# Sliding-window attention and a gated FFN: split float32r scores from unit 16 on, raw weights in buffers of their own

## The chip, the cores and the metric

The kernel runs on one core of a Trainium2 chip. The metric is device time in microseconds of one launch, median of three runs. TensorE is called PE in the profile (PEld is its weight load), VectorE DVE, ScalarE ACT, GpSimd POOL, SyncE SP. Each engine runs its own list of instructions in order; SP issues most of the DMA transfers and holds up those behind one that waits.

## The reference

Attention over four batches of 8 heads, 768 positions and 64 dimensions, with 8 global keys and a window of 96, then one FFN on its output with a rational activation. The weights come as float64.

```python
scores = scale * np.matmul(q, k.transpose(0, 1, 3, 2))
...
bias = -slopes[:, None, None] * dist[None, :, :]
scores = np.where(keep, scores + bias, -1e9)          # keep: global or in the window
a = softmax(scores)
x = np.matmul(a, v)                                   # (3072 tokens, 512)
...
h = x @ w_in                                          # (512, 2048)
g = (a0 + a1*h + a2*h**2 + a3*h**3) / (1 + |b0|*|h| + |b1|*h**2 + 1e-6)
return g @ w_out                                      # (2048, 512)
```

## The kernel before

**Units.** The work of attention is cut into 96 units: 128 queries of two heads. Unit u belongs to chunk `c = u // 8` of 256 tokens; eight units, two rows of 128 queries (t = 0, 1) by four head pairs (p = 0 to 3), make a chunk. A row's keys are its own 128 and the 128 before, with the global keys copied into the first 8 columns of the older block. Row i is 0 to 5 in a batch, so units 0 to 23 are the first batch, and units 16 to 23 are its rows 4 and 5.

**Two forms of scores.** Units below `PLAIN` (24) compute in float32: two transposes on PE (`tk`, q and k of a head pair, L389), ACT copies them to `qz` and `kF` (L402, L404), two float32 matmuls give the scores (`s`, L433). From unit 24 on every operand is split into two float32r parts. `st_move` (L147) sends the loaded q and k of two units through a DMA into a float32r tile `mv`; PE transposes it (L383); ACT writes the rounded half of each head into `kq` (L415) and DVE the remainder (L416) into the other half of the partitions; two DMAs turn the halves of q around (`qT`, L420 and L421); then four float32r matmuls give the scores (L438). The keys of the row before are kept in `kF` or in `kq`, the global keys in `kGF` or `kG`.

**After the scores.** DVE takes masked scores with their maximum (`pr`, L452), ACT the exponential, DVE the sums (L467, L469), POOL multiplies by the reciprocal (L478); PE transposes the probabilities (`tp`, L494), ACT or DVE copies them to `pT`; PE multiplies by v (`o`, L520), and ACT and DVE write the result into `xh` and `xl`. For units from 24 on, the probabilities pass through one more DMA (`pm`) and are transposed in float32r.

**FFN.** It is cut into 96 tiles f of 256 of the 2048 columns by 256 tokens, eight to a chunk. Tiles 0 to 7 (chunk 0) use float32 matmuls (`h` at L263, `acc` at L342), the others three float32r matmuls for each product (L271, L347), with weights split into a high part (`hi`, ACT or DVE) and a low part (`win_l`, `wout_l`, mostly POOL, L223). The activation of a tile is `st_ew1` to `st_ew4`: ACT's `fu`, `fa`, `fs`, DVE's polynomial (L302, L303), POOL's sum (L304), ACT's logarithm and exponential (L311, L312), and DVE's last three steps L316, L317, L318, after which PE may accumulate it.

**Weights.** A piece of 128 rows by 512 weights arrives as float64 (512 KB, `fetch`, L183) in a buffer r, and `decode` makes float32 of it in four steps: ACT (L202), POOL (L206), DVE twice (L207, L209). There are 32 pieces, in the order of the table `WSCHED`. Six raw buffers: three in the pool `early`, three that belong to tag g, which the FFN uses later.

**Order.** The loop over steps t writes each stage with a priority out of the tables `PRI` and `PRI_A`, and a scheduler orders each engine's list by these priorities and its own estimates. FFN tile f stands at step `turn(f)`: f + 10 up to f = 16, then slowly up to f + 13. At t = `PLAIN` the pool `early` is closed and the pool of the split form opened in its place.

Of the kernel before, what the change touches and what calls it, by code (L numbers as in the profile page):

```python
# [18 lines left out]
P = 128  # L19
G = 8  # L20
# [6 lines left out]
EARLY_LAG = 10  # L27
F2 = 2
# [6 lines left out]
PLAIN = 24  # L35
# [71 lines left out]
def tile_kernel(ctx: ExitStack, tc: tile.TileContext, q, k, v, n_global, n_local,  # L107
# [49 lines left out]
    wout_l = const.tile([P, NFT, DM], FR, name="wout_l")  # L157
# [8 lines left out]
    def w_lo(key):  # L166
        if key[0]:
            return win_l[:, key[1], key[2] * 2 * TOK:(key[2] + 1) * 2 * TOK]
        return wout_l[:, key[1], :]
# [225 lines left out]
    def st_qkE(u):  # L395
# [14 lines left out]
        raw = tk.bitcast(F32)  # L410
        half = float(2.0 ** (p - 1))
        for x in range(2):
            own, other = slice(x * D, (x + 1) * D), slice((1 - x) * D, (2 - x) * D)
            at = kq[:, 2 * p + x, i % 2:3:2 - i % 2, :]
            nc.scalar.activation(out=at[own], in_=raw[own], func=AF.Copy, scale=half)  # L415
            nc.vector.scalar_tensor_tensor(out=at[other], in0=raw[own], scalar=half, in1=at[own], op0=ALU.mult,  # L416
                                           op1=ALU.subtract)
        hs = slice(2 * p, 2 * p + 2)
        qT = pl.late.tile([P, 2, P], FR, tag="qT", name=f"qT{u}", bufs=4)
# [51 lines left out]
    def st_norm(u):  # L471
        if u < DIVIDED:
            return
        i = unit(u)[4]
        pr, st = prob[u]
        for x in range(2):
            d = blocks_of(pr[:, x], i)
            nc.gpsimd.tensor_scalar(  # L478
                out=d, in0=d, scalar1=st[:, 6 + x:7 + x], scalar2=None, op0=ALU.mult)
        if u >= PLAIN:  # L480
            own = (lambda y: y) if i else (lambda y: y[:, :, 0, :])
            moved = pl.late.tile([P, 2, 2, P], FR, tag="pm", name=f"pm{u}", bufs=2)
            nc.sync.dma_start(out=own(moved).bitcast(F32), in_=own(pr))
            prob[u] = (moved, st)

    def st_pT(u):
# [3 lines left out]
        kind, unit_r = (FR, ident_r) if u >= PLAIN else (F32, ident)  # L490
# [9 lines left out]
    def run_of(u):  # L500
        return 4 if u >= PLAIN else 2
# [26 lines left out]
    def st_x(u0):  # L528
# [16 lines left out]
        if u0 < DIVIDED:  # L545
            rs = pl.early.tile([P, 2, P], F32, tag="rs", name=f"rs{u0}", bufs=1)
            nc.scalar.copy(out=rs, in_=r)
            nc.vector.tensor_tensor(out=o, in0=o, in1=rs, op=ALU.mult)
# [7 lines left out]
    def windowed(lates):  # L556
# [3 lines left out]
        pl.kF = pl.early.tile([P, NPAIR, 2, P], F32, name="kF")  # L560
# [278 lines left out]
```

## Time and profile before

| | |
|---|---|
| runs | 749.71, 750.93, 751.01 us; median 750.93 |
| profiled execution | 749.57 us, of it span 747.8 us |
| mean granted PE clock | 0.996 |
| busy share of the span | PE 97%, PEld 84%, DVE 80%, ACT 77%, POOL 61% |
| DMA | 79.49 MB, 0.9 or more busy in the first 40 us, 0.3 to 0.5 from 160 to 660 us |

Busy shares are means over stages that differ: up to some 90 us weights are fetched and decoded, while attention of the first two chunks and the float32 tiles of the FFN run; weights are split up to some 180 us; then all chunks look alike up to 660 us, and the rest is FFN alone. A row of the chain is a start, a length, the engine, the tile and the line. A timeline row has in brackets how long the engine idled before it, and what ended that.

### The profile page before, as it was taken

To read this page: it belongs to the slowest core of one execution; us is meant where nothing else is said; L and a number is where in the kernel's file an instruction comes from. 1 tells how busy PE (TensorE), PEld (TensorE's weight loads), DVE (VectorE), ACT (ScalarE), POOL (GpSimd) and SP (SyncE) were. 2 spreads that over 40 slices of the span, in tenths; PEclk is the share of its full clock that TensorE was granted. 3 is DMA by queue.
4 is the path that set the end of the run, shared out by engine and by line. 5 is a ranking of instruction groups with operands and counts; after the bars stand their busy time and mean duration, and the time that the engine had idled before them with its cause. 6 is when DMAs were issued, how large, how long until landed. Compare 5 with 4: busy or idle time off the path is not lost.

```text
span 747.8 us, 15330 instructions
## 1 busy us (share of the span) xinstructions
PE 724.8 (97%) x5026; PEld 629.7 (84%) x5026; DVE 601.3 (80%) x1437; ACT 577.1 (77%) x1303; POOL 457.3 (61%) x504
## 2 busy tenths in 40 slices
PE   6798999999999999999999999999999999999996
PEld 4575667888988989998999999998998989998994
DVE  6889975888889897888888888887888888875664
ACT  6898576877977886877887878877877878866764
POOL 3385996776576675655665657656666566664441
PEclk9999999999999999999999999999999999999999
DMA  9986101123534443334334334334434333210000
GB/s 264 299 285 224 43 22 23 50 58 100 142 106 132 146 117 90 114 107 109 111 100 114 114 103 124 116 101 100 123 91 123 117 91 102 77 48 1 29 1 33
DMA packets 123581, 79.49 MB, mean 106 GB/s; under 512 B 82532, under 2 KB 104036, under 8 KB 123492
## 3 DMA queue, kind: packets, MB, share of 16 engines
q1 hardware_dynamic: 122432, 78.15, 36.4%
q8 instruction: 42, 0.69, 0.4%
q10 hardware_dynamic: 1060, 0.26, 0.2%
q14 instruction: 47, 0.39, 0.2%
HBM read 35.92 MB, written 6.29 MB: 56 GB/s over the span
## 4 chain that ended last, share of the span: by engine, by line
PE 87%; DVE 4%; ACT 4%; DMA 2%; issue 1%; POOL 0%; SPq 0%; DVEq 0%; ACTq 0%; POOLq 0%
PE h L271 34%; PE acc L347 32%; PE o L520 5%; PE s L438 5%; PE tp L494 3%; PE acc L342 2%; DMA r<-in_moe_w_in_dram 2%; PE s L433 2%; PE h L263 2%; PE tk L383 1%; ACT pr L462 1%; ACT m L202 1%; DVE pr L452 1%; PE tk L389 0%; ACT fa L296 0%
## 5 line engine op out<-in xcount | busy, mean ns | idle before, releaser
L478 POOL TENSOR_SCALAR pr<-pr,stats 128x256 f32<-128x256 f32 (+1 forms) x176 | 157.0, 903 | 74.0 <-DVE stats L469 47.2
L271 PE MATMUL h<-xh,win_l 128*128 128x256 f32 x704 | 198.2, 282 | 0.0
L304 POOL TENSOR_TENSOR fa<-fa,fs 128x512 f32<-128x512 f32 x95 | 123.8, 1303 | 98.4 <-ACT fs L297 88.0
L347 PE MATMUL acc<-wout_l,g 128*128 128x512 f32 x352 | 139.3, 396 | 0.0
L327 POOL TENSOR_TENSOR g<-fu,g 128x512 fp32r<-128x512 f32 x87 | 114.0, 1311 | 34.3 <-ACT g L326 22.9
L271 PEld LDWEIGHTS h<-xh,win_l 128*128 128x128 f32 x704 | 133.1, 189 | 2.1 <-issue 1.2
L295 ACT ACTIVATE fu<-h,coef 128x512 f32<-128x512 f32 (+1 forms) x97 | 75.1, 774 | 46.4 <-PE h L271 40.9
L462 ACT ACTIVATE pr<-pr,stats 128x256 f32<-128x256 f32 (+1 forms) x192 | 92.9, 487 | 16.8 <-DVE stats L452 16.0
L311 ACT ACTIVATE fs<-fa,coef 128x512 f32<-128x512 f32 (+1 forms) x97 | 69.6, 718 | 30.2 <-POOL fa L304 28.7
L316 DVE SCALAR_TENSOR_TENSOR fu<-fu,coef,q 128x512 f32<-128x512 f32 (+1 forms) x97 | 71.6, 738 | 25.0 <-ACT q L312 23.5
L302 DVE TENSOR_TENSOR fu<-fu,h 128x512 f32<-128x512 f32 (+1 forms) x97 | 65.7, 678 | 30.9 <-ACT fs L297 28.2
L347 PEld LDWEIGHTS acc<-wout_l,g 128*128 128x128 f32 x352 | 66.2, 188 | 11.9
L415 ACT ACTIVATE kq<-tk 64x256 fp32r<-64x256 f32 x144 | 54.3, 377 | 26.5 <-DVE kq L416 15.4
L303 DVE SCALAR_TENSOR_TENSOR fu<-fu,coef,h 128x512 f32<-128x512 f32 (+1 forms) x97 | 71.7, 739 | 1.9
L317 DVE SCALAR_TENSOR_TENSOR q<-fa,coef,q 128x512 f32<-128x512 f32 (+1 forms) x97 | 72.1, 744 | 0.0
L497 DVE COPY pT<-tp 128x512 f32<-128x512 f32 (+1 forms) x75 | 48.4, 645 | 24.9 <-PE tp L494 24.1
L416 DVE SCALAR_TENSOR_TENSOR kq<-tk,kq 64x256 fp32r<-64x256 f32 x144 | 60.9, 423 | 8.7 <-ACT kq L415 4.4
L318 DVE SCALAR_TENSOR_TENSOR fu<-q,fu 128x512 f32<-128x512 f32 (+1 forms) x97 | 66.1, 682 | 1.6
L297 ACT ACTIVATE fs<-h,coef 128x512 f32<-128x512 f32 (+1 forms) x97 | 66.3, 683 | 1.4 <-DVE fu L318 1.1
L296 ACT ACTIVATE fa<-h,coef 128x512 f32<-128x512 f32 (+1 forms) x97 | 65.6, 676 | 0.5 <-DMA out_dram<-o 0.5
L326 ACT CAST g<-fu 128x512 fp32r<-128x512 f32 (+1 forms) x89 | 54.9, 617 | 8.3 <-DVE fu L318 7.6
L312 ACT ACTIVATE q<-fs 128x512 f32<-128x512 f32 (+1 forms) x97 | 57.3, 591 | 1.7 <-DVE fu L318 0.7
(258 smaller groups left out, 2005.6 us busy)
## 6 DMA issues: line engine op xcount, KB each, us to landing
pm<-pr SPq DMA_DIRECT2D x60, 256.0 KB
mv<-nat SPq DMA_DIRECT2D x36, 256.0 KB
qT<-kq SPq DMA_DIRECT2D x144, 64.0 KB
r<-in_moe_w_in_dram SPq DMA_DIRECT2D x16, 512.0 KB
r<-in_moe_w_out_dram SPq DMA_DIRECT2D x16, 512.0 KB
nat<-in_q_dram SPq DMA_DIRECT2D x48, 128.0 KB
vt<-in_v_dram SPq DMA_DIRECT2D x48, 128.0 KB
out_dram<-o SPq DMA_DIRECT2D x24, 256.0 KB
```

The source lines that it names most:

```text
L271: nc.tensor.matmul(out=hps[f][:, y, :], lhsT=w[:, fs], rhs=x[:, ct, :], start=(n == 0), stop=(n == 3 * NCT - 1))
L295: nc.scalar.activation(out=u, in_=h, func=AF.Identity, scale=a3, bias=a2)
L297: nc.scalar.activation(out=s, in_=h, func=AF.Square, scale=b1)
L303: nc.vector.scalar_tensor_tensor(out=u, in0=u, scalar=a1, in1=h, op0=ALU.add, op1=ALU.mult)
L304: side(f).tensor_tensor(out=a, in0=a, in1=s, op=ALU.add)
L311: nc.scalar.activation(out=s, in_=a, func=AF.Ln, bias=q1)
L316: nc.vector.scalar_tensor_tensor(out=u, in0=u, scalar=a0, in1=r, op0=ALU.add, op1=ALU.mult)
L317: nc.vector.scalar_tensor_tensor(out=r, in0=a, scalar=q1, in1=r, op0=ALU.add, op1=ALU.mult)
L327: side(f).tensor_tensor(out=g[:, 1, ys], in0=u, in1=g[:, 0, ys], op=ALU.subtract)
L347: nc.tensor.matmul(out=acc, lhsT=gs[f][:, z, y, ts], rhs=w, start=(ft == 0 and n == 0), stop=(ft == NFT - 1 and n == 2))
L462: nc.scalar.activation(out=d, in_=d, func=AF.Exp, scale=-1.0, bias=st[:, x:x + 1], accum_out=st[:, 2 + 2 * x:3 + 2 * x])
L478: nc.gpsimd.tensor_scalar(out=d, in0=d, scalar1=st[:, 6 + x:7 + x], scalar2=None, op0=ALU.mult)
```

## The change

`PLAIN` is now 16: scores in float32 end after the second row pair of the first batch, and units 16 to 23 use the split form. `MOVED` (24) keeps their probabilities in float32, with their transposes at t - 3 and PV at t - 4. Units 16 to 19 find the keys of the row before in `kF` and split these too (`apart` on `kF`, and a copy of the global keys to `kG`). `turn` spreads its three extra steps as one over tiles 8 to 16 and two over tiles 16 to 24. The pool `share` holds seven buffers of 4 KB a partition for raw weights, which later hold the low parts of w_out, two 128-row blocks each; the eighth pair lies where `kF` was. Raw weights no longer use the g buffers. `MOVED` takes the place of `PLAIN` in the same way in `st_norm` (shown), `st_pT` and `run_of`. A branch that no unit took (in `st_x`) is gone.

```diff
+LATER = ((1, 1), (2, 2))
-PLAIN = 24
+PLAIN = 16
+MOVED = 24
...
-    wout_l = const.tile([P, NFT, DM], FR, name="wout_l")
+    share = ctx.enter_context(tc.tile_pool(name="share", bufs=1))
+    wout_l = {}
...
     def w_lo(key):
-        return wout_l[:, key[1], :]
+        n, m = divmod(key[1], 2)
+        if n not in wout_l:
+            wout_l[n] = shared("k" if n == NFT // 2 - 1 else "s", [P, 2, DM], FR, f"wout_l{n}")
+        return wout_l[n][:, m, :]
+
+    def shared(tag, shape, dt, name):
+        return share.tile(shape, dt, tag=tag, name=name, bufs=1 if tag == "k" else NFT // 2 - 1)
...
-        home = (pl.early, "raw", 3) if (len(full) + len(fetched)) % 6 in (1, 3, 5) else (pl.ffn, "g", pl.gbufs)
-        raw = home[0].tile([P, 2, 2, TOK], F32, tag=home[1], name="r" + "_".join(map(str, key)), bufs=home[2])
+        raw = fetched[key] = shared("s", [P, 2 * TOK, 2], F32, "r" + "_".join(map(str, key)))
...
+        def apart(raw, at):
+            half = float(2.0 ** (p - 1))
+            for x in range(2):
+                own, other = slice(x * D, (x + 1) * D), slice((1 - x) * D, (2 - x) * D)
+                y = at(2 * p + x)
+                nc.scalar.activation(out=y[own], in_=raw[own], func=AF.Copy, scale=half)
+                nc.vector.scalar_tensor_tensor(out=y[other], in0=raw[own], scalar=half, in1=y[own], op0=ALU.mult,
+                                               op1=ALU.subtract)
+        if u < PLAIN + NPAIR:
+            apart(pl.kF[:, p, 1 - i % 2, :], lambda h: kq[:, h, 1 - i % 2, :])
+            nc.gpsimd.tensor_copy(out=pl.kG[:, hs, :], in_=kq[:, hs, 1 - i % 2, 0:G])
+        apart(tk.bitcast(F32), lambda h: kq[:, h, i % 2:3:2 - i % 2, :])
...
-        if u >= PLAIN:
+        if u >= MOVED:
...
-        pl.kF = pl.early.tile([P, NPAIR, 2, P], F32, name="kF")
+        pl.kF = shared("k", [P, NPAIR, 2, P], F32, "kF")
...
-            return f + EARLY_LAG + (LAG - EARLY_LAG) * min(max(f - 2 * FPC, 0), FPC) / FPC
+            return f + EARLY_LAG + sum(n * min(max(f - c * FPC, 0), FPC) / FPC for c, n in LATER)
...
             if t - 2 < PLAIN:
                 on("pT", st_pT, t - 2)
+            elif PLAIN <= t - 3 < MOVED:
+                on("pT", st_pT, t - 3)
...
+            elif t % 2 == 0 and PLAIN <= t - 4 < MOVED:
+                pv(t - 4, 700)
```

Three places in the engines' lists. First DVE while weights are decoded, around the end of FFN tile 1 (names: w1_2_3f is a piece of w_in, w0_10f one of w_out, r its raw form, fu1 and q1 tile 1). Before:

```order
L207 SCALAR_TENSOR_TENSOR w1_2_3f_875<-w1_2_3f_875,r1_2_3_876 128x512
L316 SCALAR_TENSOR_TENSOR fu1_671<-fu1_671,coef_63,q1_747 128x512
L317 SCALAR_TENSOR_TENSOR q1_747<-fa1_672,coef_63,q1_747 128x512
L209 SCALAR_TENSOR_TENSOR w1_0_3f_795<-r1_0_3_796,w1_0_3f_795 128x512
L302 TENSOR_TENSOR fu2_756<-fu2_756,h2_736 128x512
L209 SCALAR_TENSOR_TENSOR w1_1_3f_802<-r1_1_3_803,w1_1_3f_802 128x512
L467 TENSOR_REDUCE stats_64<-stats_64 128x2
L209 SCALAR_TENSOR_TENSOR w1_2_3f_875<-r1_2_3_876,w1_2_3f_875 128x512
L207 SCALAR_TENSOR_TENSOR w1_3_3f_882<-w1_3_3f_882,r1_3_3_883 128x512
L318 SCALAR_TENSOR_TENSOR fu1_671<-q1_747,fu1_671 128x512
```

And now, on the same engine:

```order
L214 SCALAR_TENSOR_TENSOR w1_3_3f_882<-w1_3_3f_882,r1_3_3_883 128x512
L323 SCALAR_TENSOR_TENSOR fu1_673<-fu1_673,coef_65,q1_747 128x512
L324 SCALAR_TENSOR_TENSOR q1_747<-fa1_674,coef_65,q1_747 128x512
L216 SCALAR_TENSOR_TENSOR w1_0_3f_795<-r1_0_3_796,w1_0_3f_795 128x512
L479 TENSOR_REDUCE stats_66<-stats_66 128x2
L216 SCALAR_TENSOR_TENSOR w1_1_3f_802<-r1_1_3_803,w1_1_3f_802 128x512
L214 SCALAR_TENSOR_TENSOR w0_10f_946<-w0_10f_946,r0_10_947 128x512
L216 SCALAR_TENSOR_TENSOR w1_2_3f_875<-r1_2_3_876,w1_2_3f_875 128x512
L216 SCALAR_TENSOR_TENSOR w1_3_3f_882<-r1_3_3_883,w1_3_3f_882 128x512
L309 TENSOR_TENSOR fu2_756<-fu2_756,h2_736 128x512
```

Piece 3_3 moved ahead of tile 1's last three steps, and its second half, the first half of w0_10, the two masked maxima of unit 13 and the first half of w0_11 now stand between L324 and tile 1's last step (L325), which follows these.

Second, PE at the accumulation of FFN tile 5 (`acc0` with `fu5`). Before:

```order
L263 MATMUL h6_1064<-x0_281,w1_2_3f_875 128x256
L263 MATMUL h6_1064<-x0_281,w1_3_3f_882 128x256
L263 MATMUL h7_1138<-x0_281,w1_0_3f_795 128x256
L263 MATMUL h7_1138<-x0_281,w1_1_3f_802 128x256
L263 MATMUL h7_1138<-x0_281,w1_2_3f_875 128x256
L263 MATMUL h7_1138<-x0_281,w1_3_3f_882 128x256
L433 MATMUL s16_1127<-kF_95,qz_97 128x256 x2
L389 MATMUL tk17_1143<-ident_65,nat16_720 128x128 x2
```

Two rows further on stands the accumulation. Now:

```order
L390 MATMUL tk16_1079<-ident_r_68,mv16_1072 128x128 x4
L506 MATMUL tp14_1133<-ident_67,pr14_964 128x128 x4
L349 MATMUL acc0_1_778<-w0_6f_706,fu3_840 128x512
L349 MATMUL acc0_1_778<-w0_7f_714,fu3_840 128x512
L270 MATMUL h7_1162<-x0_283,w1_0_3f_795 128x256
L270 MATMUL h7_1162<-x0_283,w1_1_3f_802 128x256
L270 MATMUL h7_1162<-x0_283,w1_2_3f_875 128x256
L349 MATMUL acc0_0_768<-w0_10f_946,fu5_991 128x512
```

The score block of unit 16 and the second transposes of the pair are gone from here, and the accumulation of tile 5 stands two h matmuls sooner.

Third, DVE ahead of that tile's last steps. Before:

```order
L302 TENSOR_TENSOR fu5_993<-fu5_993,h5_973 128x512
L467 TENSOR_REDUCE stats_64<-stats_64 128x2
L318 SCALAR_TENSOR_TENSOR fu4_925<-q4_984,fu4_925 128x512
L303 SCALAR_TENSOR_TENSOR fu5_993<-fu5_993,coef_63,h5_973 128x512
L469 RECIPROCAL stats_64<-stats_64 128x2
L222 CAST w1_0_1h_1199<-w1_0_1f_322 128x512
L316 SCALAR_TENSOR_TENSOR fu5_993<-fu5_993,coef_63,q5_1075 128x512
```

And now:

```order
L309 TENSOR_TENSOR fu5_991<-fu5_991,h5_971 128x512
L644 TENSOR_SCALAR halves_1068<-masks_70 128x384
L644 TENSOR_SCALAR half0_1069<-mask0_69 128x128
L425 SCALAR_TENSOR_TENSOR kq_1066<-kF_97,kq_1066 64x128 x3
L310 SCALAR_TENSOR_TENSOR fu5_991<-fu5_991,coef_65,h5_971 128x512
L425 SCALAR_TENSOR_TENSOR kq_1066<-kF_97,kq_1066 64x128 x4
L229 CAST w1_0_1h_1215<-w1_0_1f_324 128x512
L425 SCALAR_TENSOR_TENSOR kq_1066<-kF_97,kq_1066 64x128
```

The eight subtractions that split the keys of the row before, and the halving of the masks, came in ahead of tile 5's last three steps.

More of the change, by code (lines that the diff above doesn't have):

```diff
@@ L179, in fetch @@
         src = w_in_i[r, 4 * j * TOK:4 * (j + 1) * TOK] if z else w_out_i[r, :]
-        home = (pl.early, "raw", 3) if (len(full) + len(fetched)) % 6 in (1, 3, 5) else (pl.ffn, "g", pl.gbufs)
-        raw = home[0].tile([P, 2, 2, TOK], F32, tag=home[1], name="r" + "_".join(map(str, key)), bufs=home[2])
-        raw = fetched[key] = raw.rearrange("p z a b -> p (z a b)").rearrange("p (f w) -> p f w", w=2)
+        raw = fetched[key] = shared("s", [P, 2 * TOK, 2], F32, "r" + "_".join(map(str, key)))
         eng.dma_start(out=raw.bitcast(I32), in_=src.rearrange("p (f w) -> p f w", w=2))
@@ L409, in st_qkE @@
         kq = pl.kq
[L410 to L417, printed above, removed]
-        hs = slice(2 * p, 2 * p + 2)
+        hs = slice(2 * p, 2 * p + 2)
+        def apart(raw, at):
[10 more added lines that the diff above has]
+        apart(tk.bitcast(F32), lambda h: kq[:, h, i % 2:3:2 - i % 2, :])
         qT = pl.late.tile([P, 2, P], FR, tag="qT", name=f"qT{u}", bufs=4)
@@ L489, in st_pT @@
         W = 2 if i else 1
-        kind, unit_r = (FR, ident_r) if u >= PLAIN else (F32, ident)
+        kind, unit_r = (FR, ident_r) if u >= MOVED else (F32, ident)
         t_ps = pl.ps_t.tile([P, 2, 2, P], kind, tag="t", name=f"tp{u}")
@@ L500, in run_of @@
     def run_of(u):
-        return 4 if u >= PLAIN else 2
+        return 4 if u >= MOVED else 2
     def st_pv(u0):
@@ L544, in st_x @@
         xh, xl = xT[c]
[L545 to L548, printed above, removed]
         nc.scalar.copy(out=xh[:, ps, cs], in_=o)
@@ L642, in windowed @@
                 on("split", st_move, t + 2)
-            if t - 4 >= PLAIN:
+            if t - 4 >= MOVED:
                 on("qkT", st_pT, t - 4, more=-5)
-            if t % 4 == 0 and t - 8 >= PLAIN:
+            if t % 4 == 0 and t - 8 >= MOVED:
                 pv(t - 8, 0)
```

## The prediction, made before the changed kernel ran

> **What bounds the kernel now.** I read the page's busy line and the chain that ended last, then the chain in order of time, then the busy time by stretches of 4 and 20 us, and last PE's and DVE's instructions in the stretches where the chain leaves PE.
>
> ```profile
> PE 724.8 (97%) x5026; PEld 629.7 (84%) x5026; DVE 601.3 (80%) x1437; ACT 577.1 (77%) x1303; POOL 457.3 (61%) x504
> PE 87%; DVE 4%; ACT 4%; DMA 2%; issue 1%; POOL 0%; SPq 0%; DVEq 0%; ACTq 0%; POOLq 0%
> 730.35 10.50 PE acc L347 x44
> ```
>
> In the chain in order of time every piece from 91.63 us on is PE's, up to the last accumulation at 730.35. From there on a microsecond less on PE is a microsecond less of the span, provided that nothing PE waits for comes later. Before 91.63 the chain goes through weight transfers, ACT and DVE.
>
> ```profile
> 68.00:72.00 4.00, 0.72 (x2) 0.48 (x3) 4.00 (x11) 3.27 (x9) 1.92 (x3) 1.00 0.67 231
> 72.00:76.00 4.00, 4.00 (x6) 1.52 (x6) 4.00 (x7) 3.77 (x9) 3.46 (x3) 0.57 0.53 207
> 96.00:100.00 4.00, 4.00 (x23) 2.78 (x23) 2.56 (x6) 2.81 (x7) 4.00 (x4) 1.00 0.01 2
> ...
> 100.00:120.00 20.00, 20.00 (x93) 13.15 (x92) 13.18 (x31) 13.67 (x32) 16.07 (x17) 1.00 0.12 27
> 120.00:140.00 20.00, 20.00 (x139) 16.64 (x138) 14.36 (x33) 17.40 (x41) 12.99 (x14) 1.00 0.17 48
> 140.00:160.00 20.00, 20.00 (x133) 17.08 (x132) 16.38 (x37) 16.48 (x41) 14.83 (x13) 1.00 0.15 34
> 220.00:240.00 20.00, 19.60 (x145) 17.09 (x145) 18.79 (x51) 16.30 (x39) 14.31 (x17) 1.00 0.42 116
> ```
>
> Columns: stretch and its length, then PE, PEld, DVE, ACT, POOL busy, granted clock, DMA share, GB/s. After 40 us PE is idle for long in one place only, 67.6 to 71.3 us, while DVE is full. Where units 16 to 23 run (98 to 165 us) PE is full and DVE has 16 us of 60 free.
>
> **The change part by part.** 1. Scores of units 16 to 23 on PE. Each had two fp32 score matmuls and two fp32 transposes; now four fp32r matmuls, and four fp32r transposes for a pair of units. The chain in order of time gives the price that PE really paid, neighbours overlapped:
>
> ```profile
> 103.63 0.86 PE s L433 x4
> 104.49 0.22 PE tk L389 x2
> 111.53 1.06 PE s L433 x4
> 149.78 0.37 PE tk L389 x2
> 162.64 1.06 PE s L433 x4
> 168.83 0.29 PE tk L383 x4
> 178.35 0.67 PE s L438 x4
> 187.60 0.48 PE s L438 x4
> ```
>
> From 103.63 to 162.64 stand the eight score blocks, four of 0.86 and four of 1.06: 7.68. Their transposes are seven of 0.22 and one of 0.37: 1.91. Together 9.59. The first split units show 0.67 where fp32 work stands ahead of the block and 0.48 between fp32r work. In the changed order five of the eight blocks have fp32 work (PV, or accumulation of the first chunk) just ahead: 5 x 0.67 + 3 x 0.48 = 4.79, and 4 x 0.29 = 1.16 of transposes. Gain 9.59 - 5.95 = 3.6, ends 3.1 (all at 0.67) and 4.6 (all at 0.48).
>
> 2. Weight staging. Raw pieces get seven buffers of their own instead of six shared ones (three of them the g buffers), so a transfer waits for the decode seven pieces back, not six. What that meets:
>
> ```profile
> 60.52 4.14 DMA r<-in_moe_w_in_dram
> ...
> 52.62 0.68 DVE L209 SCALAR_TENSOR_TENSOR w_6f<-r,m 128x512 int32<-128x512 int32 x1
> 58.95 0.70 DVE L207 SCALAR_TENSOR_TENSOR m<-m,r 128x512 int32<-128x512 int32 x1 [1.24 <-ACT m L202]
> 65.85 0.75 DVE L317 SCALAR_TENSOR_TENSOR q<-fa,coef,q 128x512 f32<-128x512 f32 x1
> 70.55 0.68 DVE L318 SCALAR_TENSOR_TENSOR fu<-q,fu 128x512 f32<-128x512 f32 x1
> ...
> 71.28 1.36 PE L342 MATMUL acc<-w_2f,fu 128*128 128x512 f32 x2 [3.64 <-DVE fu L318]
> 72.44 1.91 PE L342 MATMUL acc<-w_3f,fu 128*128 128x512 f32 x2
> 74.14 1.68 PE L342 MATMUL acc<-w_2f,fu 128*128 128x512 f32 x2
> 82.21 3.72 PE L263 MATMUL h<-x,w_2f 128*128 128x256 f32 x16 [0.55 <-DVE fu L303]
> 91.63 1.12 PE L342 MATMUL acc<-w_6f,fu 128*128 128x512 f32 x2 [0.18 <-DVE fu L318]
> ```
>
> The transfer at 60.52 (piece 3_3) can start some 7 us sooner, since the piece that it then waits for (w_6, started at 52.62) is decoded by 53.3. But the transfers are not what PE waits for at 67.6: that is the last step of FFN tile 1 (fu, L318), which DVE reaches at 70.55 because decode steps stand between it and L317 at 65.85. With data sooner, the order puts more decoding there: both halves of 3_3, the first halves of w_10 and w_11, and the masked maximum of a unit. By the rows below and above (0.68 a decode step, 0.42 a maximum, busy) three steps and two maxima are 2.9 at most; they overlap a little, and I count 2.5 us later. Against it stand the 1.24 us that DVE waited for ACT's first decode step at 57.7, since ACT now does two pieces (r_5, r_6) ahead of FFN tile 0 and not behind it: net 1.3 us more idle PE at 71. The work so moved is missing later: the waits of 0.55 and 0.18 us go. I take +0.5 for the stage. Ends: +2.5 (DVE starts no sooner, nothing given back) and -1.4: at 91.63 PE waits on DVE again, so PE cannot be there sooner than DVE, which has the 1.24 to give, and 0.18 of wait.
>
> 3. The change-over, now at step 16 on a fuller DVE. DVE gets two subtractions for each of eight units, and eight half-size ones that split the keys of the row before (kF); ACT gets their other halves.
>
> ```profile
> L416 DVE SCALAR_TENSOR_TENSOR kq<-tk,kq 64x256 fp32r<-64x256 f32 x144 | 60.9, 423 | 8.7 <-ACT kq L415 4.4
> L452 DVE CUSTOM_DVE_ANT_0 pr<-s,masks 128x256 f32<-128x256 f32 x100 | 40.5, 420 | 17.6 <-PE s L438 8.8 <-POOL pr L478 3.5 <-PE s L433 3.1
> L452 DVE CUSTOM_DVE_ANT_0 pr<-s,mask 128x128 f32<-128x128 f32 x20 | 5.6, 288 | 4.2 <-PE s L438 2.4 <-PE s L433 1.7
> L209 DVE SCALAR_TENSOR_TENSOR w_3f<-r,m 128x512 int32<-128x512 int32 x1 | 0.7, 680 | 0.0
> L209 DVE SCALAR_TENSOR_TENSOR w_3f<-r,w_3f 128x512 int32<-128x512 int32 x4 | 4.0, 998 | 0.0
> L402 ACT ACTIVATE qz<-tk 64x128 f32<-64x128 f32 x48 | 12.9, 269 | 8.0 <-PE tk L389 7.6
> L415 ACT ACTIVATE kq<-tk 64x256 fp32r<-64x256 f32 x144 | 54.3, 377 | 26.5 <-DVE kq L416 15.4
> L636 DVE TENSOR_SCALAR half<-mask 128x128 bf16<-128x128 bf16 x1 | 0.4, 382 | 0.0
> 98.33 0.69 DVE L222 CAST w_1h<-w_1f 128x512 fp32r<-128x512 f32 x1 [1.44 <-POOL win_l L223]
> 100.59 0.68 DVE L318 SCALAR_TENSOR_TENSOR fu<-q,fu 128x512 f32<-128x512 f32 x1
> 104.98 1.02 PE L342 MATMUL acc<-w_10f,fu 128*128 128x512 f32 x2
> ```
>
> DVE: 16 x 0.423 = 6.8, and 8 x 0.29 (a 128-element pass of DVE) = 2.3: 9.1 us on 43.9 of the 60 from 100 to 160, which shrink to about 56: 94%. In 220:240 DVE is at 18.79 of 20, the same 94%, and PE loses 0.4 of 20. So it is covered, thinly. ACT: 2 x 0.377 a unit for three of about 0.27 is no more, the keys are 8 x 0.27 = 2.2 more, on 13.67 to 17.40 of 20: covered, as are POOL's dozen small copies. The SP queue gets four moves of 256 KB and sixteen of 64 KB where DMA stands at 12 to 17%. What SP holds behind them are loads of two steps ahead. The score that needs the moved queries stands 9.5 us behind its transposes in the rows above (168.83 to 178.35), and by counted rows 10 to 11 us in the changed order, so that cover stays.
>
> The place where this is thin is the last step of FFN tile 5. It ended at 101.2 and PE used it at 104.98: 3.8 to spare. In the changed order two h matmuls (0.46 each, 3.72 for eight), a score block (1.06) and a pair of transposes (0.22) less stand on PE between the accumulations of tile 3 (91.63) and of tile 5, so it comes 2.2 sooner. DVE has the two mask halvings (0.38 at most each, 0.7; they stood at step 24) and the 2.3 of keys in front of it, less the 1.44 that it idled at 97: 1.6 later. 3.8 - 2.2 - 1.6 is nothing to spare, and a key subtraction can be held up by POOL (998 against 680 above: 0.32 each, 2.5 in all). PE's own 1.3 of lateness from part 2 covers half of that. I take 0.7 of stall; ends 0 and 6 (third rival).
>
> 4. FFN turns: tiles 9 to 15 come up to one step later, tiles 17 to 23 end at the same lag of 13. PE has the same FFN work, and the end (730.35 on) is the same order. Probabilities still go in fp32 until unit 24, one step later than before, so transposes and PV of units 16 to 23 cost what they cost. Nothing taken, with half a microsecond either way for the new order.
>
> Sum: -3.6 + 0.5 + 0.7 = -2.4. The profiled execution took 749.57 (span 747.8 and 1.8 around it); it would take 747.2. The median shown is 750.93, 1.36 above it, so I forecast 748.5 against that median. Differences under 0.2% (1.5 us) are about what measuring this kernel cannot tell from none.
>
> **The rivals.** First, more gain. If the idle stretch at 71 shrinks instead, PE also keeps its clock: 72:76 shows 0.57, and three accumulation pairs there took 0.34, 0.89 and 0.66 longer than the 1.02 of the one at 104.98, 1.9 together. But DVE's step ahead of 91.63 caps the stage at -1.4: -3.6 - 1.4 + 0.3, 746.2. For it speaks that weights land sooner, against it DVE's order. The Trainium skill (TensorE: Matmul & The Clock Gate, Part 1) has the clock halve after an idle window of about 3.4 us. By that rule, and this trace agrees with 3.64 us idle and 0.57, a stall cut by a quarter microsecond would give PE back the whole 1.9 at once, and the sum would be the same 746.2, by the cap.
>
> Second, no change: DVE at 94% lets PE wait several times between 98 and 165 us, as the 0.4 in 220:240, but with the weight splits on top. Six steps at 0.4 are 2.4 on top of the forecast: 750.9.
>
> Third, slower, by one mechanism: the eight key subtractions read two SBUF operands while POOL is full (4.00 of 4 at 96 to 100). The decode rows show what that can do: 680 ns with one operand in PSUM, 998 on average with both in SBUF, and the longest 1.43 us.
>
> ```profile
> 74.09 1.43 DVE L209 SCALAR_TENSOR_TENSOR w_3f<-r,w_3f 128x512 int32<-128x512 int32 x1
> ```
>
> At 0.75 more each, 8 x 0.75 = 6 us stand ahead of tile 5's last step, and PE stalls 6: -3.6 + 0.5 + 6 = +2.9, 753.8. It turns the sign at about 0.4 us for each. The Trainium skill (SBUF — State Buffer, Who interferes with whom) says that a DVE instruction with two SBUF inputs waits out a GpSimd instruction that reads SBUF. By it each of the eight could wait out most of a POOL instruction; the 998 agrees that some do.
>
> **How the numbers follow.** Forecast 0.45 (747.0 to 749.4: part 1 at its ends, the rest as taken, and the unseen half microsecond), first rival 0.21 (744.9 to 747.0), second 0.22 (749.4 to 752.4), third 0.12 (above). Faster 0.66, same 0.22, slower 0.12. The range 745.2 to 752.2 leaves out the third rival and the edges of the others; the forecast's own is 747.0 to 749.4.
>
> **What would show it.** Step 1: s and tk of units 16 to 23 in the chain at 0.48 to 0.67 and 0.29. Step 2: PE's wait for FFN tile 1's last step at 4 to 6 us, raw transfers no longer waiting for w_7. Step 3: DVE near 94% from 100 to 160 and PE's wait at the accumulation of tile 5 under 1 us; the key subtractions at 0.3, not 1 us. I am wrong if PE waits several times after 98 us, if the stall at 71 goes, or if the chain from there on is not PE.

## The result, and the profile after

The changed kernel takes 755.72 us (median of 6 runs) against 750.55 us for the kernel before (6 runs): a ratio of 1.0067, with a 95% interval of 1.0055 to 1.0079, so 4.1 to 5.9 us slower. The profiled execution took 755.09 us, its span is 753.2, 5.4 more than before. I had forecast 748.5, in 745.2 to 752.2.

First the page's busy line and the chain that ended last:

```profile
PE 721.0 (96%) x5026; PEld 629.0 (84%) x5026; DVE 613.8 (81%) x1459; ACT 581.2 (77%) x1305; POOL 458.3 (61%) x508
PE 72%; DVE 9%; ACT 6%; POOL 5%; issue 4%; DMA 2%; SPq 0%; POOLq 0%; DVEq 0%; ACTq 0%
```

PE is busy 3.8 us less than before (724.8): the saving is there. But PE's part of the chain fell from 87% to 72%, and the span grew. So PE idles 9.2 us more (753.2 - 721.0 = 32.2 against 23.0). Three stretches say where. The columns are stretch, length, busy time of PE, PEld, DVE, ACT and POOL, granted clock, DMA share, GB/s; first before, then after:

```profile
0.00:60.00 60.00, 48.96 (x272) 36.14 (x273) 45.09 (x152) 48.88 (x146) 30.08 (x59) 1.00 0.88 275
60.00:98.00 38.00, 33.63 (x138) 20.95 (x136) 36.73 (x73) 26.97 (x62) 29.37 (x27) 0.96 0.36 115
98.00:260.00 162.00, 161.40 (x1112) 137.22 (x1112) 132.41 (x323) 130.59 (x306) 112.75 (x120) 1.00 0.33 89
```

```profile
0.00:60.00 60.00, 47.02 (x261) 34.80 (x262) 44.70 (x150) 46.62 (x141) 29.39 (x58) 1.00 0.90 281
60.00:98.00 38.00, 30.41 (x128) 19.84 (x127) 35.81 (x67) 26.38 (x59) 27.20 (x26) 0.91 0.33 104
98.00:260.00 162.00, 157.67 (x1068) 132.98 (x1067) 141.38 (x342) 130.26 (x300) 114.08 (x122) 1.00 0.36 96
```

Length less PE's busy time gives idle PE: 11.04, 4.37 and 0.60 us before, 12.98, 7.59 and 4.33 now. That is +1.9 at the start, +3.2 around the stall at 70 us, +3.7 where units 16 to 23 and the chunks after them run; the rest of the span adds 0.3. With the 3.8 saved on PE this is the 5.4 of the spans.

The stall at 70 us has doubled. In the timeline of the changed kernel, DVE's last three steps around it (L324, L325 are the L317, L318 of before), the decode step that DVE waited for, and PE's wait in brackets:

```profile
61.38 0.70 DVE L214 SCALAR_TENSOR_TENSOR m<-m,r 128x512 int32<-128x512 int32 x1 [1.18 <-ACT m L209]
69.34 0.74 DVE L324 SCALAR_TENSOR_TENSOR q<-fa,coef,q 128x512 f32<-128x512 f32 x1
76.36 0.68 DVE L325 SCALAR_TENSOR_TENSOR fu<-q,fu 128x512 f32<-128x512 f32 x1
77.09 2.08 PE L349 MATMUL acc<-w_2f,fu 128*128 128x512 f32 x2 [6.96 <-DVE fu L325]
```

From the end of L324 (70.08) to L325 DVE now works 6.3 us on other things; before it was 3.95 (66.60 to 70.55). L324 itself is 3.5 us later, and 2.2 of these stand already at the last step of FFN tile 0 (58.29, before 56.11). So tile 1's last step comes 5.8 us later, and since PE arrives 2.5 later itself (70.13 against 67.64), its wait is 3.3 longer. Behind it PE has a longer stretch of low clock:

```profile
72.00:76.00 4.00, 0.00 (x0) 0.00 (x0) 4.00 (x10) 1.75 (x5) 1.83 (x2) 0.87 0.78 291
76.00:80.00 4.00, 2.91 (x4) 1.36 (x5) 4.00 (x8) 3.47 (x9) 3.47 (x3) 0.50 0.27 107
80.00:84.00 4.00, 4.00 (x13) 2.10 (x12) 4.00 (x8) 0.00 (x0) 3.84 (x4) 0.77 0.02 4
```

Half of PE's 2.91 us and 0.23 of the 4.00 are lost, 2.4 in sum, against 0.43 x 4 = 1.7 before. That the longer wait made this stretch longer is not shown: below, kernels with the old wait have the long stretch as well.

After 98 us the waits are many and small. The three largest in the changed kernel (engine, line, waited for; us in total, times, longest):

```profile
PE o L532 <- ACT pT L509: 1.4, 1, 1.4
PE h L278 <- DVE xl L558: 1.2, 1, 1.2
PE h L278 <- DVE fu L310: 0.9, 1, 0.9
```

### The profile page after: what moved, and what is told of

The parts are those of the page before. It is cut to its first block, busy times and chain, and to the rows that moved or that the text cites. A ratio compares the mean times of both kernels' runs of the same rounds, so it can differ in the third digit from the quotient of the medians.

```text
span 753.2 us, 15445 instructions
## 1 busy us (share of the span) xinstructions
PE 721.0 (96%) x5026; PEld 629.0 (84%) x5026; DVE 613.8 (81%) x1459; ACT 581.2 (77%) x1305; POOL 458.3 (61%) x508
## 4 chain that ended last, share of the span: by engine, by line
PE 72%; DVE 9%; ACT 6%; POOL 5%; issue 4%; DMA 2%; SPq 0%; POOLq 0%; DVEq 0%; ACTq 0%
PE h L278 30%; PE acc L354 28%; PE s L450 5%; PE o L532 4%; PE tp L506 3%; POOL fa L311 2%; PE tk L390 1%; ACT pr L474 1%; DVE fu L323 1%; DVE q L324 1%; POOL pr L490 1%; DVE kq L425 1%; DMA r<-in_moe_w_in_dram 1%; POOL win_l L230 1%; PE s L445 1%
## 5 line engine op out<-in xcount | busy, mean ns | idle before, releaser
L318 ACT ACTIVATE fs<-fa,coef 128x512 f32<-128x512 f32 (+1 forms) x97 | 69.6, 718 | 27.5 <-POOL fa L311 26.0
L424 ACT ACTIVATE kq<-tk 64x256 fp32r<-64x256 f32 x160 | 60.4, 378 | 37.2 <-DVE kq L425 24.0
L323 DVE SCALAR_TENSOR_TENSOR fu<-fu,coef,q 128x512 f32<-128x512 f32 (+1 forms) x97 | 71.5, 738 | 20.0 <-ACT q L319 17.7
L425 DVE SCALAR_TENSOR_TENSOR kq<-tk,kq 64x256 fp32r<-64x256 f32 x160 | 67.6, 422 | 11.4 <-ACT kq L424 6.4
L324 DVE SCALAR_TENSOR_TENSOR q<-fa,coef,q 128x512 f32<-128x512 f32 (+1 forms) x97 | 72.1, 743 | 0.0
L325 DVE SCALAR_TENSOR_TENSOR fu<-q,fu 128x512 f32<-128x512 f32 (+1 forms) x97 | 66.2, 683 | 1.8
```

The costliest lines, as they stand in the source:

```text
L318: nc.scalar.activation(out=s, in_=a, func=AF.Ln, bias=q1)
L323: nc.vector.scalar_tensor_tensor(out=u, in0=u, scalar=a0, in1=r, op0=ALU.add, op1=ALU.mult)
L324: nc.vector.scalar_tensor_tensor(out=r, in0=a, scalar=q1, in1=r, op0=ALU.add, op1=ALU.mult)
L425: nc.vector.scalar_tensor_tensor(out=y[other], in0=raw[own], scalar=half, in1=y[own], op0=ALU.mult, op1=ALU.subtract)
```

## Experiments

Three theories. *Staging*: seven raw buffers pull decode work ahead of FFN tile 1 on DVE. *Change-over*: the split of units 16 to 23 makes a fuller DVE that PE has to wait for. *Order*: whatever an edit is for, it makes the scheduler draw the engines' lists anew, and the lists of the kernel before are hard to equal. The times of before in these comparisons are 750.0 to 750.4.

### Which part costs

staging_alone is the changed kernel with the old scores and turns:

```diff
-LATER = ((1, 1), (2, 2))
-PLAIN = 16
+LATER = ((2, 3),)
+PLAIN = 24
...
-        if u < PLAIN + NPAIR:
+        if u < PLAIN + NPAIR and i:
```

> The weight staging of the changed kernel (seven buffers shared with the low parts of w_out) with float32 scores up to unit 24 and FFN turns as before. DVE's list is the same as in the changed kernel for its first 217 rows. Staging theory: the changed kernel is late because DVE reaches the last step of FFN tile 1 some 6 us later, PE's wait there is 6 to 8 us instead of 3.6, and the clock is halved for longer; then this kernel alone is slower than before by 5 to 8 us (755 to 759), and more than the changed kernel since nothing is saved on scores. Change-over theory: the loss comes from PE's waits between 132 and 250 us in the changed kernel (about 4 us) because DVE is full there; then this kernel is within 2 us of before.

split_alone is the changed kernel with six buffers again, every second one a g buffer:

```diff
-        raw = fetched[key] = shared("s", [P, 2 * TOK, 2], F32, "r" + "_".join(map(str, key)))
+        if (len(full) + len(fetched)) % 6 in (1, 3, 5):
+            raw = shared("s", [P, 2, 2, TOK], F32, name)
+        else:
+            raw = pl.ffn.tile([P, 2, 2, TOK], F32, tag="g", name=name, bufs=pl.gbufs)
...
-... bufs=1 if tag == "k" else NFT // 2 - 1)
+... bufs=3 if tag == "s" else 1)
```

> Split scores from unit 16, with FFN turns of the changed kernel, but raw weights staged as before: six buffers, every second one a g buffer of the FFN (the low parts of w_out take over the other three later). DVE's list is the same as in the kernel before for its first 185 rows. Staging theory: PE waits 3.6 us for FFN tile 1 as before, and the score gain shows: 745.5 to 748, 3 to 5 us faster than before. Change-over theory: the waits between 132 and 250 us are still there, 3 to 4 us in sum, and eat the gain: 749 to 752.

turns_alone is the kernel before with the new turns:

```diff
-            return f + EARLY_LAG + (LAG - EARLY_LAG) * min(max(f - 2 * FPC, 0), FPC) / FPC
+            return f + EARLY_LAG + min(max(f - FPC, 0), FPC) / FPC + 2 * min(max(f - 2 * FPC, 0), FPC) / FPC
```

> The kernel before with only the FFN turns of the changed kernel (one extra step over tiles 8 to 16, two over tiles 16 to 24). Both theories above take this part as nothing: 750 to 751.5. A third theory, that later turns leave PE without FFN work between 132 and 150 us, expects waits of 1 us or more there and 752 or more.

Measured: staging_alone 756.00, ratio 1.0080 (1.0067 to 1.0093), 6 us slower; split_alone 750.37, 1.0005 (0.9995 to 1.0015), no change; turns_alone 750.14, 0.9995 (0.9987 to 1.0004), no change. In these three the whole loss goes with the staging, and the split gains nothing; how much of it is only a new order is taken up below. Both theories were half right. In staging_alone the loss lies ahead of 98 us, as its windows and its one long wait show:

```profile
0.00:60.00 60.00, 46.74 (x272) 35.05 (x273) 45.36 (x152) 49.24 (x146) 30.75 (x60) 1.00 0.89 283
60.00:98.00 38.00, 30.79 (x130) 18.93 (x128) 37.11 (x71) 26.48 (x61) 28.10 (x26) 0.87 0.35 101
74.92 2.08 PE L349 MATMUL acc<-w_2f,fu 128*128 128x512 f32 x2 [7.21 <-DVE fu L325]
```

Idle PE is 13.26 + 7.21 there against 11.04 + 4.37: 5.1 us more, and the spans differ by 4.9 (752.7 and 747.8). In split_alone PE is busy 720.4, 4.4 less than before, and gives it back in waits, of which these are three (timeline, wait in brackets; line numbers shift by a few between kernels, and L330 here is the last step of an FFN tile):

```profile
83.72 1.12 PE L354 MATMUL acc<-w_4f,fu 128*128 128x512 f32 x2 [1.72 <-DVE fu L330]
135.19 0.66 PE L537 MATMUL o<-pT,vt 128*64 128x128 f32 x8 [1.10 <-ACT pT L514]
238.40 0.54 PE L511 MATMUL tp<-ident_r,pm 128*128 128x128 f32 x4 [0.80 <-DVE stats L469]
```

### What in the staging costs

Fewer buffers of their own: in six_buffers the ring has six, in five_buffers five, the other low parts of w_out on tags of their own.

```diff
-... bufs=1 if tag == "k" else NFT // 2 - 1)
+... bufs=5 if tag == "s" else 1)
```

> The changed kernel with six buffers of its own for raw weights instead of seven. In DVE's list 13 rows stand between the second and the third of the last steps of FFN tile 1, against 12 in the changed kernel and 6 in the kernel before. If the order of decode steps behind earlier transfers is what costs, and not the number of buffers, it is as slow as the changed kernel: 754 to 757. If the seventh buffer alone pulls the work ahead, it is at 747 to 750.

> The changed kernel with five raw buffers of its own. In DVE's list two decode steps fewer stand between the last two steps of FFN tile 1 than with seven buffers: 3.0 us of work instead of 5.8. If that order is what costs, the wait for tile 1 is 3 to 4 us and the time 750 to 752. If fewer buffers only make the weights late, 754 or more.

Measured: six_buffers 754.65, 1.0055 (1.0040 to 1.0070); five_buffers 751.20, 1.0016 (1.0006 to 1.0027), which is where the order of decode steps had put it. Its wait for tile 1 is shorter than in the kernel before:

```profile
69.96 1.54 PE L349 MATMUL acc<-w_2f,fu 128*128 128x512 f32 x2 [3.07 <-DVE fu L325]
```

Up to 98 us PE idles 15.77 us with five buffers, against 15.41 in the kernel before and 20.57 in the changed kernel; from 98 to 260 it idles 4.59, as in the changed kernel (4.33). So the ring and the new homes as such need not cost much ahead of 98 us; one or two buffers more do, with the order they bring. But the theory of the wait for tile 1 holds only in part: six_buffers has the time that it gave, and waits only 3.93 us for tile 1, and another 2.42 for POOL's product `pr` at 86.17.

Is it tile 1's last step? changed_short_tile1 and split_short_tile1 leave out the two steps behind L323 for this tile.

```diff
+        if f != 1 or pl.split:
             nc.vector.scalar_tensor_tensor(out=r, in0=a, scalar=q1, in1=r, op0=ALU.add, op1=ALU.mult)
             nc.vector.scalar_tensor_tensor(out=u, in0=r, scalar=2.0, ...)
```

> The changed kernel, with FFN tile 1's activation ending at DVE's first product: the two correcting steps after it (the Newton step on the reciprocal) are left out for this one tile of 96, so its columns are less exact. Staging theory: PE's wait of 7.0 us for this tile goes to 2 us or less, its clock stays whole at 76 to 82 us, and the kernel gains 5 to 8 us: 748 to 751. Rival (the lateness sits in DVE as a whole, so the next tile's steps are as late): the wait only moves to FFN tile 2 and the gain is 2 us or less, 753.5 or more.

> The split from unit 16 with the staging of before, FFN tile 1 shortened in the same way (two correcting steps left out for that tile). Staging theory: the wait of 3.66 us and the stretch of half clock behind it go, 745 to 747 against 750.4 of the split alone. Rival: DVE's lateness moves to tile 2 (its wait of 1.7 grows by what tile 1's shrinks), 749 or more.

Measured: 759.22, 1.0126 (1.0110 to 1.0142), and 756.88, 1.0101 (1.0084 to 1.0118). Less work, and 3.5 and 6.5 us slower than with it. The rival's times held and so did its main point, that the wait only moves; but it moves further than to FFN tile 2, in one kernel to attention, and neither theory had a loss. The wait for tile 1 is gone in both, and a wait of over 5 us stands elsewhere, first in changed_short_tile1, then in split_short_tile1:

```profile
91.95 2.50 PE L270 MATMUL h<-x,w_3f 128*128 128x256 f32 x5 [5.48 <-DVE fu L310]
88.88 0.69 PE L512 MATMUL tp<-ident,pr 128*128 128x128 f32 x2 [5.28 <-POOL pr L496]
```

The step that PE waits for at 70 us is thus a symptom: from 64 to 92 us DVE has no idle time in most of these kernels (28.00 of 28 us busy before, 27.84 in the changed kernel), decode steps take the room, and some step of the FFN or of attention is late.

Why did transfers that land sooner not help DVE, as I had counted on? Piece w_7 is the last that is built in a bank of PSUM, the memory into which this kernel's matmuls write, and its bank, r, is also that of q of FFN tile 0. So its first decode step cannot run before that tile's last one, however early the raw weights lie there. changed_free_w7 and split_free_w7 build it in SBUF; before_free_w7 does so in the kernel before.

```diff
-BANKS = "hrhaa" * 2 + "raa" * 3 + "r" + " " * 12
+BANKS = "hrhaa" * 2 + "raa" * 3 + " " * 13
```

> The changed kernel, in which piece w_7 (the 20th to be decoded) is built in its own SBUF buffer and not in PSUM bank r, which FFN tile 0 holds until its last step. Theory A: DVE's idle time of 5 us between 48 and 64 us is decode work held up behind tile 0 by that bank, so earlier transfers cannot help; freed, DVE has two to three pieces done before 60 us, its full stretch from 64 to 92 us ends 1.5 to 2.5 us sooner, and PE's wait for tile 1 shrinks by as much: 751 to 753.5 against 755.7. Theory B: decode steps that come sooner only push the steps of FFN tile 0 and 1 back again (in DVE's list four decode steps now stand ahead of tile 0's first one): 755 or more.

> The split alone (staging of before) with the same change for piece w_7. Here the freed steps come in behind tile 0's and tile 1's first steps. Theory A: the 1.2 us that DVE idles at 57.7 are used, tile 1's last step comes 1 to 2 us sooner: 747.5 to 749.5 against 750.4. Theory B: 750 or more.

> The kernel before, with piece w_7 outside PSUM bank r. Where raw weights come late, as here and in the split alone, the freed decode steps of w_7 to w_9 only go ahead of the steps of FFN tiles 0 and 1: 752 to 757 by theory order and by the split's result. If DVE's 1.24 us of idle time at 57.7 can be used at all, 748.5 to 750.

Measured: changed_free_w7 752.61, 1.0041 (1.0025 to 1.0058), 3.1 us better than the changed kernel; split_free_w7 756.60, 1.0078 (1.0053 to 1.0102); before_free_w7 758.57, 1.0110 (1.0090 to 1.0130). In the changed kernel the steps came as theory A has them: DVE's busy time from 48 to 64 us, first changed, then with w_7 freed, and the wait for tile 1 in the latter.

```profile
48.00:64.00 16.00, 16.00 (x87) 13.10 (x86) 10.96 (x25) 14.51 (x33) 12.81 (x17) 1.00 0.49 148
48.00:64.00 16.00, 13.82 (x77) 10.87 (x76) 15.40 (x26) 13.12 (x27) 13.19 (x13) 1.00 0.76 238
72.72 1.12 PE L349 MATMUL acc<-w_2f,fu 128*128 128x512 f32 x2 [3.12 <-DVE fu L325]
```

DVE has 10.96 of 16 us of work with the bank shared and 15.40 without, and the wait for tile 1 shrinks from 6.96 to 3.12. The gain in time does not follow from that. Stretches of changed_free_w7:

```profile
0.00:60.00 60.00, 45.18 (x264) 33.53 (x265) 49.89 (x154) 49.25 (x147) 31.69 (x58) 1.00 0.97 310
60.00:98.00 38.00, 31.14 (x119) 19.30 (x118) 35.06 (x63) 23.88 (x54) 27.32 (x26) 0.91 0.21 60
98.00:260.00 162.00, 159.66 (x1092) 134.99 (x1091) 139.74 (x345) 130.05 (x301) 110.35 (x121) 1.00 0.37 98
```

Up to 98 us PE idles 14.82 + 6.86 = 21.68 us, more than the changed kernel's 20.57, since other waits took the room (the longest 2.88, for `xl` at 86.76). Only behind 98 us it idles less, 2.34 against 4.33. So the step was right, and by these rows it was luck that the time came out in theory A's range. And the same edit costs 6 and 8 us where the staging is the old one. Nor do the two edits that helped add up: five_buffers_free_w7 joins them.

> The changed kernel with five raw buffers and with piece w_7 outside PSUM bank r. Singly these gave 751.2 and 752.6 against 755.7. If DVE's idle time before 64 us and the order of decode steps are two separate causes, they add up: 747 to 749.5, better than both kernels. If both act by filling the same idle time (with five buffers DVE idles only 1.5 us between 48 and 64 us), it is at 750.5 to 753.

Measured: 756.03, 1.0073 (1.0057 to 1.0089), worse than either.

The start. Before, q and k of unit 12 were issued on SP at 36.79; now five raw transfers stand ahead of them:

```profile
36.79 0.38 SPq L141 DMA_DIRECT2D nat<-in_q_dram  x1
```

```profile
35.70 6.40 SPq L190 DMA_DIRECT2D r<-in_moe_w_out_dram  x5
42.21 0.38 SPq L143 DMA_DIRECT2D nat<-in_q_dram  x1
```

changed_loads_on_act moves these loads to ACT's queue.

```diff
+        other = nc.scalar if u in (12, 14) else other
-        nc.sync.dma_start(out=n[:, 0], ...)
+        (other if u in (12, 14) else nc.sync).dma_start(out=n[:, 0], ...)
```

> The changed kernel, in which q and k of units 12 to 15 are loaded by ACT's DMA queue, so that they no longer stand behind five raw transfers on SP's (35.7 to 42.2 us). If those loads are why PE idles 2.1 us more than before between 36 and 60 us, and why FFN tile 0 ends 2.2 us later, then tile 0 ends at 57 us and the time is 752.5 to 754.5. If the transfers themselves (the DMA engines are busy throughout) or the order of DVE hold PE, it stays at 755 to 757.

Measured: 763.76, 1.0185 (1.0171 to 1.0199). It is inconclusive on the question: PE's idle time from 36 to 48 us rose to 2.9 us from 2.2, FFN tile 0 ended at 60.8 instead of 59.0. The loads stand in ACT's list now, where I take it that they hold what is behind them; that was not tested. Whether SP's order makes the 1.9 us of the start stays open.

### Why the split alone gains nothing

Five edits of split_alone. split_no_key_split has POOL copy the keys of the row before instead of splitting them:

```diff
-            apart(pl.kF[:, p, 1 - i % 2, :], lambda h: kq[:, h, 1 - i % 2, :])
+            for x in range(2):
+                nc.gpsimd.tensor_copy(out=kq[:, 2 * p + x, 1 - i % 2, :], in_=pl.kF[:, p, 1 - i % 2, :])
```

> The split alone, in which the keys of the row before (kF) are not split for units 16 to 19 but copied whole by POOL, so that these units' scores count them in a wrong form; DVE loses eight passes of 0.32 us and ACT eight of 0.30. If the change-over's own passes make PE wait after 98 us: the waits at 135 and 180 us shrink and it is at 747.5 to 749. If they are covered, as the prediction had it, and the waits come from the full DVE of the regular split: 750 to 751.

split_low_on_pool:

```diff
-LO_V = (13, 15, 17, 19, 21, 23, 25, 27, 29, 31)
+LO_V = ()
```

> The split alone, with all 32 low parts of the weights subtracted on POOL; ten of them were on DVE, between 100 and 185 us, where they take 0.7 to 1.3 us each, about as much as the split of units 16 to 23 adds to DVE there. If the waits after 98 us (1.1 at 135, 0.7 at 180, 0.8 at 238 us) come from DVE being full, they go and the gain on scores shows: 747 to 749. If POOL, at 13 to 18 of 20 us, becomes the one that is waited for: 750 to 753.

split_later_turns, split_later_pv and split_from_20, one line each:

```diff
-LATER = ((1, 1), (2, 2))
+LATER = ((1, 2), (2, 1))
...
-                pv(t - 4, 700)
+                pv(t - 4, 1700)
...
-PLAIN = 16
+PLAIN = 20
```

> The split alone, with FFN turns two extra steps over tiles 8 to 16 and one over tiles 16 to 24 (one and two before), so that tiles 9 to 23 stand up to one step later. Theory distance: in the split alone PE meets results of DVE and ACT that are barely late (1.10 for pT, 0.71 for h and xl, 0.80 for stats), because it does its part of a step faster; one more step between FFN and attention takes the waits from 130 to 200 us away: 747.5 to 749.5. Theory load (DVE's work per step limits PE, wherever they meet): 750 to 751.5.

> The split alone, with the PV of units 16 to 23 one step later. Theory distance: the wait of 1.10 us for ACT's pT at 135 us goes, and if nothing takes its place 749 to 750; FFN tile 16, which needs the last of these units, then waits for xl instead (0.42 at 181 us grows to 1 us or more). Theory load: 750 to 751.5.

> The split alone, from unit 20 instead of 16: half of the units, so half of PE's saving (2.2 us) and half of DVE's extra passes (4.6 us). Theory load: PE's waits after 80 us halve as well and the time stays with before, 749.5 to 751. Theory distance: the waits at 135 us, ahead of unit 20, go first, and half of the saving shows: 747.5 to 749.

| kernel | us | ratio (interval) |
|---|---|---|
| split_no_key_split | 751.64 | 1.0015 (1.0005 to 1.0026) |
| split_low_on_pool | 753.78 | 1.0051 (1.0039 to 1.0063) |
| split_later_turns | 752.29 | 1.0026 (1.0016 to 1.0035) |
| split_later_pv | 755.75 | 1.0059 (1.0037 to 1.0081) |
| split_from_20 | 753.74 | 1.0043 (1.0029 to 1.0057) |

None comes out faster than the split alone, whatever it relieves, and each has a different set of waits. With PV a step later PE waits for other things than the ones that went (2.3 and 1.4 us for qT). With half of the units split it waits 2.90 us in one place where it did not wait at all before. Neither DVE's load nor the distance between the engines, as forecast, explains that: both theories of this group fell. What the five have in common is a new order; that it is the cause is argued, not shown.

### What an order is worth

before_one_copy is the control: the kernel before, with the copy of one unit's transposed probabilities on ACT instead of DVE.

```diff
-EARLY = 21
+EARLY = 22
```

> The kernel before, with the copy of one unit's transposed probabilities (unit 21) on ACT instead of DVE: 0.65 us of 600 change engines, and 1251 rows of PE's list differ, from unit 21 on. Theory order: the lists of the kernel before are a lucky draw, and any edit draws again; the time moves by 2 us or more, to 752 to 755. Theory work: only work and waits that the edit itself makes count, 750 to 751.

Measured: 756.75, ratio 1.0083 (1.0065 to 1.0101): 6.4 us slower, by one copy of 0.65 us on an engine that is not the bound. The theory that only an edit's own work and waits count is refuted by it; the order theory had expected 2 us or more. Its busy line, and its stretch after 98 us:

```profile
PE 730.3 (97%) x5026; PEld 631.6 (84%) x5026; DVE 602.8 (80%) x1435; ACT 577.2 (76%) x1305; POOL 455.6 (60%) x504
98.00:260.00 162.00, 159.75 (x1061) 133.41 (x1059) 127.79 (x306) 125.62 (x295) 109.64 (x116) 1.00 0.30 80
```

With the same instructions PE is busy 5.5 us longer than before (724.8), and from 98 to 260 us it idles 2.25 instead of 0.60. Up to 98 us it idles no more than before (its wait for tile 1 is 3.63), so its loss lies where that of staging_alone does not. By the names in the two traces the engines' instructions are the same up to some 160 us, and yet this execution is 1.7 us behind there. The same score block, before and here:

```profile
162.57 1.13 PE L433 MATMUL s<-kF,qz 128*128 128x256 f32 x4
164.31 1.13 PE L433 MATMUL s<-kF,qz 128*128 128x256 f32 x4
```

So 1.7 of the 8.2 us between the two spans (756.0 and 747.8) are a difference between executions and not of the order; the 6.5 behind it agree with the 6.4 of the medians. The longer stretch of half clock, under the same wait, explains 1.7 of the 5.5 and also lies ahead of the moved copy; what in the order makes up the other 3.8 is not settled. PE's busy time can therefore not be read as its work to better than some 4 us.

## Why the prediction was wrong

**Part 1, the scores.** Right in its rows, as far as the trace can tell. In the chain of split_alone the blocks and transposes of units 16 to 23 stand at what was forecast:

```profile
135.85 0.67 PE s L455 x4
142.56 0.47 PE s L455 x4
143.03 0.29 PE tk L395 x4
150.77 0.67 PE s L455 x4
```

PE's busy time is 3.8 us (changed) and 4.4 us (split alone) lower, the forecast 3.6; but by the control such totals also move with the order.

**Part 2, weight staging.** This is the first term that failed: forecast +0.5, at most +2.5; with staging_alone it measured 6.0 (5.0 to 7.0). The extra decode work between L324 and L325 came as counted (2.3 us, forecast 2.5). The 1.24 us set against it did not: DVE still waits 1.18 us for the same step, ACT's first on w_7. Bank r, which w_7 shares with FFN tile 0, bars that step up to tile 0's end at 58.98. From there to 60.68 it stands behind other work in ACT's list, without idle time of ACT:

```profile
58.29 0.69 DVE L325 SCALAR_TENSOR_TENSOR fu<-q,fu 128x512 f32<-128x512 f32 x1
60.22 0.60 ACT L509 COPY pT<-tp 128x512 f32<-128x512 f32 x1
60.68 0.67 ACT L209 ACTIVATE m<-r 128x512 f32<-128x512 f32 x1
```

So transfers that land sooner could not bring it forward, and the "DVE starts no sooner" of the upper end was the case. Beyond that, the lateness at the start was not in the sum at all: FFN tile 0 ends 2.2 us later, and PE idles 1.9 us more up to 60 us. The q and k loads that fell behind raw transfers may be its cause; that stays open. Nor was a longer half clock in the sum (0.7 more than before); I had seen the stall's clock only as something to gain, but whether the longer stall made it longer is not shown.

**Part 3, the change-over.** Forecast +0.7, 0 to 6. The place that I feared, the accumulation of FFN tile 5, held: PE waits for no L325 after 98 us. The key subtractions were as cheap as the forecast 0.29 (by shape; mean ns behind the busy time):

```profile
L425 DVE SCALAR_TENSOR_TENSOR kq<-kF,kq 64x128 fp32r<-64x128 f32 x8 | 2.1, 285 | 0.2
```

so the third rival, and the rule of the Trainium skill that stood beside it (SBUF — State Buffer, Who interferes with whom), did not decide here: that rule's wait is not in these 285 ns. It was hardly put to the test: from 101.2 to 103.9 us, where seven of the eight ran, POOL had only two copies of 0.2 and 0.3 us. And the 998 ns from which I priced that rival was the mean of four rows of one name; of the twelve such steps with both inputs in SBUF in the kernel before, eight took 0.68 us, as with one input in PSUM. But idle PE grew by 3.7 us between 98 and 260. Nor is DVE at the 94% that I had forecast:

```profile
100.00:120.00 20.00, 20.00 (x100) 13.80 (x95) 16.08 (x34) 13.23 (x30) 13.64 (x15) 1.00 0.30 76
120.00:140.00 20.00, 18.64 (x120) 13.99 (x119) 14.88 (x36) 15.49 (x38) 12.64 (x14) 1.00 0.32 85
140.00:160.00 20.00, 19.14 (x135) 16.54 (x136) 19.35 (x44) 17.70 (x41) 16.48 (x15) 1.00 0.28 65
```

It is busy 50.3 of 60 us, 84%, and PE waits all the same: for ACT's copy, for x, for one step of the activation. The second rival had the effect (several small waits that take the gain), but the load that it gave as the reason did not come, and relieving DVE (split_low_on_pool) did not bring the gain out.

**Part 4, the order.** "Half a microsecond either way for the new order" is the term that was mis-sized most. One copy moved costs 6.4 us here. Every one of the four parts is an edit that re-draws the lists from its place on, and I priced only the places that I had looked at. Of the 19 other orders that were run, the changed kernel's among them, none is faster than that of the kernel before, and two (turns_alone and split_alone) are level with it within their intervals; the others are 0.15 to 1.9% slower. So a new order need not cost anything, and the half microsecond was far too narrow.

**What stays open.** Whether the split from unit 16 can gain at all: no edit of it brought the 4 us of PE out, and no kernel here beats the one before. How much of the 6 us of staging_alone is the staging and how much the draw: its loss lies ahead of 98 us, in waits that come with the buffers' order, and five buffers take them back; but the control shows that losses of this size can come with a new order alone. One control is one draw, so it does not say how often.

## What to carry to other kernels

Where a scheduler writes the order of a kernel that is close to its bound, price an edit in two terms: its own work, and a new draw of the order, and measure the second with an edit that does nothing (one copy on another engine), better with several such edits, before a mechanism gets the blame or the credit. A wait that ends on a full engine can be a symptom: when its step was shortened here, the wait stood elsewhere. When an edit does what it should at its place and the time moves as forecast, look whether the time was gained at that place. And before a transfer is counted as time gained, look for what else its consumer waits for; here it was a PSUM bank shared with the stage that it should have overtaken.

## What the runs showed of the hardware

In the traces' records of the granted clock PE's half clock comes in pieces of about 3.41 us: after PE's wait of 3.6 us for tile 1 it lasted 3.41 us in the kernel before and in split_alone, and 6.83 in turns_alone and before_one_copy, with the same wait. The instructions of these last two are those of the kernel before up to there, so its length changes between executions of the same lists. Shorter waits bring it on as well. In split_from_20 it came behind 2.90 us, here by 3 us (the clock is the third number from the end):

```profile
144.91 0.44 PE L283 MATMUL h<-xh,w_2h 128*128 128x256 f32 x1 [2.90 <-DVE fu L315]
145.00:148.00 3.00, 3.00 (x15) 3.00 (x16) 2.91 (x6) 2.40 (x5) 2.58 (x3) 0.51 0.21 41
148.00:151.00 3.00, 3.00 (x23) 2.44 (x23) 2.53 (x5) 0.47 (x1) 0.28 (x1) 0.92 0.01 3
```

In five_buffers it came behind 3.07 us. So a stall shorter by 0.57 us (3.64 to 3.07) did not give the clock back there, where the first rival counted on a quarter of a microsecond. In changed_loads_on_act, on the other hand, a wait of 3.44 us brought none:

```profile
70.00:74.00 4.00, 4.00 (x6) 1.70 (x7) 4.00 (x9) 3.85 (x11) 2.88 (x3) 0.57 0.67 191
91.15 0.44 PE L507 MATMUL tp<-ident,pr 128*128 128x128 f32 x2 [3.44 <-POOL pr L491]
92.00:94.00 2.00, 2.00 (x12) 1.79 (x10) 0.57 (x2) 1.63 (x5) 2.00 (x3) 1.00 0.29 67
```

The first row is five_buffers behind its wait, the other two are changed_loads_on_act. The Trainium skill (TensorE: Matmul & The Clock Gate, Part 1) has windows of about 3.4 us that run free of the kernel. The pieces of 3.41 agree with it; that 2.90 us were enough says that the window need not be idle to its end.
